# PSUM banks as single-bank tiles, constant rows behind the first layer norm, VectorE scores from three steps ahead

## Chip, cores, metric

The kernel runs on one core of a Trainium2 chip. The metric is the device time of one launch in microseconds (us). Each kernel is run several times. The median is quoted, and ratios are taken against runs of the kernel before, made in the same rounds on the same chip.

## The reference

A pre-norm transformer block: B = 1, S = 2048, D = 640, 32 heads of 20, gated width F = 1728, all in bf16.

```python
def _A_ref(x, wqkv, wo):                       # attention
    qkv = (x @ wqkv).reshape(B, S, 3, H, Dh).transpose(2, 0, 3, 1, 4)
    q, k, v = qkv[0], qkv[1], qkv[2]
    p = softmax(einsum("bhqd,bhkd->bhqk", q, k) * Dh ** -0.5)
    o = einsum("bhqk,bhkd->bhqd", p, v)
    return o.transpose(0, 2, 1, 3).reshape(B, S, D) @ wo

def _B_ref(x, w_gate, w_up, w_down):           # gated bilinear
    return ((x @ w_gate) * (x @ w_up)) @ w_down

h   = x + _A_ref(layernorm(x), A_wqkv, A_wo)
out = h + _B_ref(layernorm(h), B_w_gate, B_w_up, B_w_down)
```

## The kernel before

It has three stretches. The **start** normalises the first 512 rows, transposes them on TensorE and projects the first K and Q. **Attention** runs over five chunks of query rows. Scores go to PSUM three or two banks at a time, and ScalarE takes their exponential. One block in eleven (186 of 2048) goes instead to VectorE, which makes an exponential in four passes with one GpSimd pass beside them. Everything else (remaining projections, the output projection, second layer norm and gated stage of the chunk before) is filled in between by a planner in Python. The planner keeps modelled clocks `pe_t`, `dve_t`, `act_t` and decides the order of instructions. The **tail** is what is left of the last two chunks when the last exponential is done.

PSUM has eight banks. Outside attention the five score banks are lent to the other work as slices of two tiles:

```python
ring = deque([dict(t=0.0), dict(t=0.0)])           # the two ordinary banks, pool mp, tag "m"

def more_banks():                                  # before the first scores and after the last
    s3 = sA.tile([P, 3, BK], F32, name="sp", tag="s3")
    s2 = sA.tile([P, 2, BK], F32, name="sp", tag="s2")
    ap = [s3[:, i, :] for i in range(3)] + [s2[:, i, :] for i in range(2)]
    for i, a in enumerate(ap):
        ring.insert(i, dict(t=pe_t, ap=a))
# ... m_take() hands out the next ring entry: such a slice, or a new tile of mp
```

The start, in order of emission (cuts marked):

```python
for t_, r_, val in ((cstk, rowk, BIAS), (cstq, rowq, 1.0)):   # constant rows of K and Q
    nc.gpsimd.memset(t_[:], 0.0)
    nc.gpsimd.memset(t_[0:1, :], val)
    for ch in range(NCH):
        nc.gpsimd.dma_start(r_[:, ch, :], t_[:])
# ...
warm_up(28)                                   # 28 matmuls on zeros
# ...
for t in range(TPC):
    ln_stats(L, t, xt[0][:, t, :])            # VectorE
ln_finish(L)                                  # VectorE, then on GpSimd: den = (var + eps) ** 0.5
nc.vector.memset(Vx[...][:, :, :, DH], 1.0)   # three fills of V
nc.vector.memset(Vx[...], 0.0)
nc.vector.memset(Vx[...], 0.0)
# ... ScalarE copies the padded K and Q weights
ln_recip(L)                                   # VectorE waits for den
lns = [ln_apply(L, t, ...) for t in range(TPC)]
more_banks()
for t in range(TPC):
    run(transposed(lns[t], lnT_dst(t)))       # TensorE into a ring bank, copied out by ScalarE or VectorE
    warm_up(1)
warm_up(2)
run(proj_pad(0, 0, 1)); run(proj_pad(0, 0, 0))
less_banks()
```

The two settings of the order:

```python
LN_SLACK = 1.0    # us that a layer-norm transpose waits, in attention, after its planned input
D_STEPS = 2       # a VectorE score block is taken at least so many steps ahead of ScalarE's
```

In the tail the gate and up weights of the last chunk's tiles 0 to 7 are loaded early into memory that Q no longer needs. Tiles 8 to 13 go through a pool of three buffers, `wst`, so tile 11 needs the buffers of tile 8.

The softmax here doesn't subtract the row's maximum and nothing guards it: scores larger than these inputs give would overflow.

Of the kernel before, what the change touches and what calls it, by code (L numbers as in the profile page):

```python
# [10 lines left out]
F32 = mybir.dt.float32  # L11
# [4 lines left out]
PSUM = bass.MemoryType.PSUM  # L16

P = 128
# [8 lines left out]
BK = 512  # L27
NCH = S // BK
# [11 lines left out]
BIAS = 127.0 * UNIT  # L40
# [2 lines left out]
EXP_A = _P2 / _P3 * 65536.0  # L43
EXP_B = _P1 / _P3 * 65536.0 ** 2
EXP_C = UNIT * _P3 / 65536.0 ** 3
LN_SLACK = 1.0
D_V = 0.72
EPS_B = 1.0013580322265625e-05

# [3 lines left out]
BANK_ACT, FIX_ACT = 0.4267, 0.056  # L53
DVE_FIX = 0.12
D_AHEAD = 1.2
D_STEPS = 2
T_TICK = 3.41
HAM = 0.50
W0, W1 = 80.0, 58.0
# [13 lines left out]
def kernel(  # L73
# [11 lines left out]
    nc = tc.nc  # L85
# [14 lines left out]
    tiny = ctx.enter_context(tc.tile_pool(name="tiny", bufs=3))  # L100
    onp = ctx.enter_context(tc.tile_pool(name="onp", bufs=1))

    sA = ctx.enter_context(tc.tile_pool(name="sA", bufs=1, space=PSUM))
    accp = ctx.enter_context(tc.tile_pool(name="accp", bufs=1, space=PSUM))
    mp = ctx.enter_context(tc.tile_pool(name="mp", bufs=2, space=PSUM))


    pe_t = 0.0
# [30 lines left out]
    def dve(us, ready=0.0):  # L139
        nonlocal dve_t  # L140
        dve_t = max(dve_t, ready) + us + DVE_FIX
        return dve_t
# [67 lines left out]
    rowk = dram.tile([32 - DH, NCH, BK], BF16, name="rowk", tag="rowk")  # L210
    rowq = dram.tile([32 - DH, NCH, BK], BF16, name="rowq", tag="rowq")
    cstk = p1.tile([32 - DH, BK], BF16, name="cstk")
    cstq = p1.tile([32 - DH, BK], BF16, name="cstq")
    for t_, r_, val in ((cstk, rowk, BIAS), (cstq, rowq, 1.0)):
        nc.gpsimd.memset(t_[:], 0.0)
        nc.gpsimd.memset(t_[0:1, :], val)
        for ch in range(NCH):
            nc.gpsimd.dma_start(r_[:, ch, :], t_[:])

    def fill_kq():  # L220
        k_src = rowk[:].rearrange("r c q -> r (c q)")
# [26 lines left out]
    def ln_stats(L, i, s, ready=0.0):  # L248
        st = tiny.tile([P, 2, 6], F32, name="st", tag="st")
        for c in range(2):  # L250
            nc.vector.bn_stats(st[:, c, :], s[:, c * HD:(c + 1) * HD])
            dve(0.34, ready)
        nc.vector.bn_aggr(L["mv"][:, i, :], st[:])
        dve(0.15)

    def ln_finish(L):
        n = L["n"]
        vb = tiny.tile([P, TPC], BF16, name="vb", tag="vb")
        nc.vector.tensor_copy(vb[:, 0:n], L["mv"][:, 0:n, 1])
        ve = tiny.tile([P, TPC], BF16, name="ve", tag="ve")  # L260
        nc.vector.tensor_scalar_add(ve[:, 0:n], vb[:, 0:n], EPS_B)
        L["pow"] = dve(0.25)
        den = tiny.tile([P, TPC], BF16, name="den", tag="den")
        nc.gpsimd.tensor_tensor(den[:, 0:n], ve[:, 0:n], half[:, 0:n], ALU.pow)
        L["den"] = den
# [14 lines left out]

    ring = deque([dict(t=0.0), dict(t=0.0)])

    def more_banks():
        s3 = sA.tile([P, 3, BK], F32, name="sp", tag="s3")
        s2 = sA.tile([P, 2, BK], F32, name="sp", tag="s2")
        ap = [s3[:, i, :] for i in range(3)] + [s2[:, i, :] for i in range(2)]
        for i, a in enumerate(ap):
            ring.insert(i, dict(t=pe_t, ap=a))

    def less_banks():  # L290
        kept = [r for r in ring if "ap" not in r]
        ring.clear()
        ring.extend(kept)

    def m_wait():
        while ring[0]["t"] > pe_t + 0.05:
            yield ("until", ring[0]["t"])

    def m_take(dt=F32, shape=None):
        rec = ring.popleft()  # L300
        rec["t"] = NEVER
        ring.append(rec)
        if "ap" in rec:
            if shape is None:
                return rec["ap"], rec
            n = shape[1] * shape[2]
            return rec["ap"].bitcast(dt)[:, 0:n].rearrange("p (a b) -> p a b", b=shape[2]), rec
        t = mp.tile(shape or [P, BK], dt, name="mt", tag="m")
        return t[:], rec

    def m_done(rec, t):
# [27 lines left out]
    def transposed(ln_t, dst):  # L339
        ln, t = ln_t  # L340
        t += LN_SLACK if attn and left else 0.0
        while t + T_SEM > pe_t + 0.05:
# [97 lines left out]
    for t in range(TPC):  # L440
        ln_stats(L, t, xt[0][:, t, :])
    ln_finish(L)
    nc.vector.memset(Vx[:, :, 0:H * VS].rearrange("p t (h e) -> p t h e", e=VS)[:, :, :, DH], 1.0)
    nc.vector.memset(Vx[:, :, H * VS:VW], 0.0)
    nc.vector.memset(Vx[:, :, (H // 2) * VS:(H // 2) * VS + DH], 0.0)
# [12 lines left out]
    run(proj_pad(0, 0, 1))  # L458
    run(proj_pad(0, 0, 0))
    less_banks()  # L460

    def first_stage():
# [232 lines left out]
    for ci, qw in enumerate(CHUNKS):  # L695
# [3 lines left out]
        for g, k0 in order:  # L699
            k1 = k0 + TPC if ci == 0 and g < NG0 else NT  # L700
            n = (k1 - k0) * qw
# [80 lines left out]
    def start_D():  # L782
        used = {j for _, j in units[-1]}
        s0 = left[0][0] + D_STEPS
        for b in left:
# [42 lines left out]
    def pump(limit):  # L828

        while dq and dve_t < limit:  # L830
            ok = [d for d in dq if d["part"] < 3 or sum(b in E_of for b in eds) < 5]
            if not ok:
                return
            c = [d for d in ok if d["ready"] <= dve_t + 0.02]
            if not c:
                nxt = min(d["ready"] for d in ok)
                if nxt >= limit:
                    return
                c = [d for d in ok if d["ready"] == nxt]
            c.sort(key=lambda d: (d["part"] != 0, -d["part"]))  # L840
            pass_D(c[0])

    def emit_PV(s):
        nonlocal acc_t
        ci, q0, qw, g, pcs = steps[s]
        need(*[("V", z[0], g // (G // 2)) for z in pcs])
        k0, k1, first, last, full = ends[s]
        if first:
            acc_t = accp.tile([P, BK], F32, name="acc", tag="acc")
        for kt, qo, n, c in pcs:  # L850
            for j in range(HP):
                h = g * HP + j
                nc.tensor.matmul(acc_t[32 * j:32 * j + 32, qo:qo + n], lhsT=Vx[:, kt, h * VS:h * VS + 32],  # L853
                                 rhs=E_of[s, j][0][:, c:c + n], start=kt == k0, stop=kt == k1 - 1,
                                 skip_group_check=len(pcs) > 1)
        for j in range(HP):
            del E_of[s, j]
        pe(0.22, "C", 512)
        if last:
            before(pe_t + T_SEM)  # L860
            if (ci, g) not in sums:

                while sum(z[3] for z in later) > 1:
                    later.pop(0)[1]()
                sums[ci, g] = npool.tile([P, BK], F32, name="accS", tag="accS")
                nc.vector.tensor_copy(sums[ci, g][:, 0:qw], acc_t[:, 0:qw])  # L866
            else:
                nc.vector.tensor_tensor(sums[ci, g][:, 0:qw], sums[ci, g][:, 0:qw], acc_t[:, 0:qw], ALU.add)
            t = dve(qw / 960, pe_t + T_SEM)
            if full:  # L870
                normalise(ci, q0, qw, g, sums.pop((ci, g)), t)
            acc_t = None
# [64 lines left out]
    n = 0  # L937
# [5 lines left out]
    def v_time(s):  # L943
        return max(t_v.get((kt, steps[s][3] // (G // 2)), NEVER) for kt, *_ in steps[s][4])

    def values(force=None):

        nonlocal pv_next, bgw
        run = 0
        while pv_next < len(steps):  # L950
            s = pv_next
            if force is not None and s > force:
                break
            if not all((s, j) in E_of for j in range(HP)):
                if force is None:
                    break
                pump(dve_t + 0.5)
                continue
            if force is None and max([E_of[s, j][1] for j in range(HP)] + [v_time(s)]) > pe_t - MARG:
                break  # L960
            if force is None and run == 0 and not ends[s][3]:

                nxt = range(s, min(s + PVS, len(steps)))
                if not all((q, j) in E_of and max(E_of[q, j][1], v_time(q)) <= pe_t + 0.3 - MARG
                           for q in nxt for j in range(HP)):
                    break
            run += 1
            emit_PV(s)
            pv_next += 1
            ci, q0, qw, g, pcs = steps[s]  # L970
            if g == G - 1 and ends[s][4]:
                while len(bg) > (ci > 0):
                    forced()
                if ci == 0:
                    open_p2()
                    bgw = 0.0
                bg.append(second_stage(ci, q0, qw, xr_of(ci, q0, qw)))
                bgw += W1 * qw / BK
                if ci == len(CHUNKS) - 2:
                    load_last()  # L980

    while n < len(units):
# [6 lines left out]
        pe_t = max(pe_t, T0)  # L989
# [3 lines left out]
        if left:  # L993
            pe_t = max(pe_t, act_t + T_SEM)
# [21 lines left out]
        while True:  # L1016
            tick()
            if not blocked and bg and (pe_t < T1 + over and credit > 0 or debt >= BK):
                c0 = cols
                c = bg_step()  # L1020
                if isinstance(c, tuple):
                    blocked = c[1] > max(T1 + over, pe_t + 0.1)
                    pe_t = pe_t if blocked else max(pe_t, c[1])
# [12 lines left out]
        pump(act_t + 0.9)  # L1036
        n += 1
    values(len(steps))
    more_banks()
    while later:  # L1040
        later.pop(0)[1]()
    end = bg.pop()
    for c in end:
# [3 lines left out]
        elif isinstance(c, tuple):  # L1047
            while bg and pe_t < c[1]:
                forced()
            pe_t = max(pe_t, c[1])  # L1050
    wst.release()
    p2s.release()
    p2.release()


# [28 lines left out]
```

## Time and profile before

| | before |
|---|---|
| median (4 runs) | 1023.13 us (1021.88 to 1023.42) |
| first exponential starts | 21.64 us |
| last exponential ends | 960.0 us |
| tail to the end of the span | 64.0 us |
| ScalarE idle, 100 to 960 us | 68 us |
| gate/up loop of the last chunk | 23.4 us |

The busy lines of the page are busy us, share of the span and instructions. The slices cut the span in 40 and give tenths. PEclk is the clock granted to TensorE.

```profile
PE 869.5 (85%) x14138; PEld 369.7 (36%) x14138; DVE 748.1 (73%) x1294; ACT 862.3 (84%) x776; POOL 222.4 (22%) x264
...
PEclk9889898879989999989999899999989998999999
```

ScalarE and TensorE are both busy about 85% of the time, which says little. The stretches have different limits, so each is read by itself. Here is the start from the timeline: start, duration, engine, line, operation, out<-in, count, and in brackets how long the engine was idle before and what ended that.

```profile
2.02 9.05 PE L238 MATMUL acc<-zeros 128*128 128x512 bf16 x28
...
8.94 2.05 POOL L218 DMA_DIRECT2D rowq<-cstq  x4 [0.29 <-POOL cstq L216]
8.99 0.17 DVE L261 TENSOR_SCALAR ve<-vb 128x4 bf16<-128x4 bf16 x1
...
10.94 0.48 DVE L443 MEMSET Vx<- 128x512 bf16 x1 [1.79 <-issue]
11.00 1.06 POOL L264 TENSOR_TENSOR den<-ve,half 128x4 bf16<-128x4 bf16 x1
...
12.31 1.51 DVE L275 TENSOR_SCALAR xw<-xw,mv,rstd 128x640 bf16<-128x640 bf16 x4
...
12.81 0.45 PE L347 MATMUL sp<-ident,xw 128*128 128x128 bf16 x5 [1.73 <-DVE xw L275]
...
14.04 0.44 PE L347 MATMUL sp<-ident,xw 128*128 128x128 bf16 x5 [0.56 <-ACT lnT L322]
...
15.14 0.69 PE L347 MATMUL sp<-ident,xw 128*128 128x128 bf16 x5 [0.44 <-DVE lnT L326]
...
18.00 1.26 PE L148 MATMUL sp<-lnT,Wp 128*32 128x512 bf16 x20
...
21.64 4.62 ACT L776 ACTIVATE E<-sp 128x1536 bf16<-128x1536 f32 x4 [5.08 <-PE sp L757]
```

Two things stand out. The variance is ready at 9.16, but its power on GpSimd (`den`) starts at 11.00, behind the DMA issues for the constant rows. And the second and the third transpose begin just after the copy of the one before it has ended (at 13.99 and 15.08), although each writes another bank. The bracket names that copy as the releaser.

The same pattern fills the tail. The first fence is the list of waits of TensorE from 957 us on (total us, times, longest us): the first five of its eleven lines. The second is four lines of TensorE's timeline in the gate/up loop.

```profile
PE sp L148 <- ACT gs L322: 2.9, 6, 0.5
PE sp L148 <- DVE hh_4766 L671: 2.5, 2, 1.9
PE sp L148 <- DVE xr L685: 1.8, 3, 0.6
PE sp L148 <- DVE rb L885: 1.3, 1, 1.3
PE sp L148 <- DVE kT_155 L624: 1.2, 2, 0.6
```

```profile
992.61 0.73 PE L148 MATMUL sp<-kT_157,qT_164 128*32 128x256 bf16 x20 [0.59 <-DVE hh_4755 L671]
993.81 1.28 PE L148 MATMUL sp<-kT_157,qT_164 128*32 128x256 bf16 x40 [0.47 <-ACT gs L322]
995.61 0.73 PE L148 MATMUL sp<-kT_157,qT_164 128*32 128x256 bf16 x20 [0.52 <-ACT gs L322]
996.15 1.28 PE L148 MATMUL mt<-kT_157,qT_164 128*32 128x256 bf16 x40
```

`sp` is a slice of one of the two shared tiles, `mt` one of the two ordinary banks. In the second fence three groups into `sp` waited about half a microsecond each for the copy out of a neighbour slice; the group into `mt` follows at once. From start to start the group at 992.61 takes 1.20 us, and the one at 995.61 takes 0.54. The Trainium skill (PSUM - Partial Sum Buffer, "PSUM bank collisions raise a hardware error") asks for semaphores by bank and quadrant. So the order between different banks is asked for by nothing but the tile that holds them.

### The profile page before, as it was taken

Reading aid. Unit: us, or ns where it says so; the run is one execution under the profiler, and the core shown is the slowest. Engines: PE = TensorE matmul, PEld = TensorE weight load, DVE = VectorE, ACT = ScalarE, POOL = GpSimd, SP = SyncE. Lnnn points to the kernel's source line nnn. Section 1 sums busy time; section 2 is a strip of 40 time slices with the busy share of each in tenths; the row PEclk is TensorE's granted clock in tenths of the full one; section 3 lists DMA queues with packets and bytes.
Section 4 is the critical chain, followed back from the end, with each engine's and each line's share of the span. In section 5 each row is a group of like instructions: output and inputs, shape, how many; then the busy total and the mean of one; then the engine's idle time right before and its main releaser. Section 6 shows DMA issues by size and latency. Waiting matters only on the chain.

```text
span 1024.0 us, 32973 instructions
## 1 busy us (share of the span) xinstructions
PE 869.5 (85%) x14138; PEld 369.7 (36%) x14138; DVE 748.1 (73%) x1294; ACT 862.3 (84%) x776; POOL 222.4 (22%) x264
## 2 busy tenths in 40 slices
PE   7778887989788889888988889899789996888886
PEld 3233233222223222223333333344334443344565
DVE  4564586858798788877787788997778896788532
ACT  3578795879899999989999999999769997999511
POOL 4000220212232222222321222232222231122000
PEclk9889898879989999989999899999989998999999
DMA  6310110101110232210011122210213305123222
GB/s 228 81 41 3 45 34 17 39 22 34 30 49 10 54 80 72 66 49 26 26 39 41 45 55 55 45 37 24 42 35 84 68 17 145 38 65 73 57 60 47
DMA packets 121916, 53.26 MB, mean 52 GB/s; under 512 B 98026, under 2 KB 117066, under 8 KB 121770
## 3 DMA queue, kind: packets, MB, share of 16 engines
q1 hardware_dynamic: 120794, 49.75, 20.1%
q8 instruction: 110, 1.80, 0.7%
q10 hardware_dynamic: 720, 1.31, 0.3%
q14 instruction: 36, 0.29, 0.1%
q0 software_dynamic: 256, 0.10, 0.0%
HBM read 43.47 MB, written 2.98 MB: 45 GB/s over the span
## 4 chain that ended last, share of the span: by engine, by line
ACT 34%; PE 26%; issue 19%; DVE 8%; DMA 6%; SPq 4%; POOL 3%; DVEq 0%; POOLq 0%; ACTq 0%
ACT E L776 34%; PE mt L148 10%; PE sp L757 7%; PE acc L853 4%; PE sp L148 3%; SPq L404 3%; DMA rb<-rd 3%; SPq L898 1%; DMA rs<-accS 1%; DVE fx L803 1%; DVE v L811 1%; POOL uc L806 1%; DVE v L809 1%; DMA rd<-rr 1%; DMA kT_157<-tmp 1%
## 5 line engine op out<-in xcount | busy, mean ns | idle before, releaser
L776 ACT ACTIVATE E<-sp 128x1536 bf16<-128x1536 f32 (+1 forms) x745 | 850.0, 1330 | 93.4 <-PE sp L757 67.1
L806 POOL TENSOR_SCALAR uc<-fx 128x512 f32<-128x512 uint16 x186 | 158.4, 852 | 553.5 <-DVE fx L803 541.7
L853 PE MATMUL acc<-E,Vx 128*32 128x256 bf16 (+3 forms) x2787 | 166.7, 324 | 6.4 <-DVE accS L866 6.4
L809 DVE SCALAR_TENSOR_TENSOR v<-fx 128x512 f32<-128x512 uint16 x186 | 151.2, 815 | 1.6
L803 DVE TENSOR_SCALAR fx<-mt 128x512 int32<-128x512 f32 x186 | 126.9, 683 | 34.0 <-PE mt L757 33.1
L811 DVE SCALAR_TENSOR_TENSOR v<-v,uc 128x512 f32<-128x512 f32 x186 | 129.4, 697 | 25.8 <-POOL uc L806 22.4
L814 DVE SCALAR_TENSOR_TENSOR ed<-fx,v 128x512 uint16<-128x512 int32 x186 | 133.1, 716 | 1.6
L853 PEld LDWEIGHTS <-Vx 128*32 128x32 bf16 x3072 | 58.9, 97 | 77.3 <-issue 72.0
L148 PE MATMUL mt<-ln2T,wu 128*32 128x512 bf16 (+1 forms) x1070 | 77.7, 365 | 1.0 <-DVE fx L803 0.6
L148 PE MATMUL mt<-ln2T,wg 128*32 128x512 bf16 (+1 forms) x1080 | 77.4, 362 | 0.7 <-DVE hh_4759 L671 0.3
L853 PE MATMUL acc<-ed,Vx 128*32 128x256 bf16 (+3 forms) x285 | 70.5, 319 | 0.9 <-DVE accS L866 0.8
L148 PE MATMUL acc<-zeros 128*32 128x512 bf16 x680 | 58.4, 398 | 0.0
L326 DVE COPY gs<-mt 128x512 f32<-128x512 f32 (+3 forms) x54 | 33.6, 622 | 11.4 <-PE mt L148 11.0
L148 PEld LDWEIGHTS <-wg 128*32 128x32 bf16 x1190 | 28.0, 96 | 31.5 <-issue 23.3
L148 PEld LDWEIGHTS <-wu 128*32 128x32 bf16 x1190 | 28.0, 97 | 31.2 <-issue 22.5
L757 PE MATMUL sp<-qT_164,kT_155 32*128 32x256 bf16 (+3 forms) x285 | 28.9, 296 | 9.8 <-ACT E L776 9.3
L866 DVE COPY accS<-acc 128x512 f32<-128x512 f32 (+2 forms) x40 | 23.3, 582 | 17.4 <-PE acc L853 15.3
L757 PE MATMUL sp<-qT_164,kT_159 32*128 32x256 bf16 (+3 forms) x290 | 27.5, 292 | 9.4 <-ACT E L776 9.0
L757 PE MATMUL sp<-qT_164,kT_157 32*128 32x256 bf16 (+3 forms) x290 | 28.0, 297 | 8.7 <-ACT E L776 8.2
L757 PE MATMUL sp<-qT_164,kT_158 32*128 32x256 bf16 (+3 forms) x287 | 28.8, 309 | 7.5 <-ACT E L776 7.2
L757 PE MATMUL sp<-qT_164,kT_156 32*128 32x256 bf16 (+3 forms) x293 | 29.3, 299 | 6.7 <-ACT E L776 6.0
L757 PE MATMUL sp<-qT_164,kT_161 32*128 32x256 bf16 (+3 forms) x290 | 28.3, 292 | 7.6 <-ACT E L776 6.7
(254 smaller groups left out, 1193.9 us busy)
## 6 DMA issues: line engine op xcount, KB each, us to landing
wg<-in_B_w_gate_dram SPq DMA_DIRECT2D x57, 160.0 KB
wu<-in_B_w_up_dram SPq DMA_DIRECT2D x57, 160.0 KB
rb<-rd SPq DMA_DIRECT2D x16, 256.0 KB
rb<-rd SPq DMA_DIRECT2D x16, 192.0 KB
out_dram<-xr SPq DMA_DIRECT2D x14, 160.0 KB
Wd<-in_B_w_down_dram SPq DMA_DIRECT2D x13, 160.0 KB
xr<-in_A_x_dram SPq DMA_DIRECT2D x2, 640.0 KB
qT_164<-in_B_w_gate_dram SPq DMA_DIRECT2D x4, 320.0 KB
```

The lines of the kernel that those rows point to most:

```text
L148: nc.tensor.matmul(out[j:j + 32], lhsT=lhsT[:, j:j + 32], rhs=rhs, start=start, stop=stop, **kw)
L326: nc.vector.tensor_copy(dst, src)
L404: nc.sync.dma_start(dst, tmp[lo - ft * P:hi - ft * P, 0:n])
L757: nc.tensor.matmul(out[:, c:c + n], lhsT=kT[g][32 * j:32 * j + 32, kt * P:(kt + 1) * P], rhs=q_of(g, q0 + qo, n)[32 * j:32 * j + 32, :], s ...
L776: nc.scalar.activation(E[:, 0:len(u), :], sp[:, 0:len(u), :], ACT.Exp, scale=LN2_ / UNIT, bias=-BIAS * LN2_ / UNIT)
L803: nc.vector.tensor_scalar_mul(fx[:], d["sp"], 512.0)
L806: nc.gpsimd.tensor_scalar(d["uc"][:], u, EXP_C, 0.0, ALU.mult, ALU.add)
L809: nc.vector.scalar_tensor_tensor(d["v"][:], d["u"], EXP_A, d["u"], ALU.add, ALU.mult)
L811: nc.vector.scalar_tensor_tensor(d["v"][:], d["v"][:], EXP_B, d["uc"][:], ALU.add, ALU.mult)
L814: nc.vector.scalar_tensor_tensor(e[:], d["fx"][:], 1.0 / 512.0, d["v"][:], ALU.mult, ALU.add)
L853: nc.tensor.matmul(acc_t[32 * j:32 * j + 32, qo:qo + n], lhsT=Vx[:, kt, h * VS:h * VS + 32], rhs=E_of[s, j][0][:, c:c + n], start=kt == k0 ...
L866: nc.vector.tensor_copy(sums[ci, g][:, 0:qw], acc_t[:, 0:qw])
```

## The change

The intent is to lend the five banks as five tiles of their own pool, which is released before the score tiles are made and made anew after the last scores; to write the constant rows after the power of the first layer norm; and to retune the two settings of the order.

```diff
-LN_SLACK = 1.0
+LN_SLACK = 2.0
-D_STEPS = 2
+D_STEPS = 3
 ...
-    sA = ctx.enter_context(tc.tile_pool(name="sA", bufs=1, space=PSUM))
 ...
-    for t_, r_, val in ((cstk, rowk, BIAS), (cstq, rowq, 1.0)):
-        nc.gpsimd.memset(t_[:], 0.0)
-        ...
+    def const_rows():
+        for t_, r_, val in ((cstk, rowk, BIAS), (cstq, rowq, 1.0)):
+            nc.gpsimd.memset(t_[:], 0.0)
+            ...
 ...
+    sA = xp = None
     def more_banks():
-        s3 = sA.tile([P, 3, BK], F32, name="sp", tag="s3")
-        s2 = sA.tile([P, 2, BK], F32, name="sp", tag="s2")
-        ap = [s3[:, i, :] for i in range(3)] + [s2[:, i, :] for i in range(2)]
-        for i, a in enumerate(ap):
-            ring.insert(i, dict(t=pe_t, ap=a))
+        nonlocal xp
+        xp = tc.alloc_tile_pool(name="xp", bufs=1, space=PSUM)
+        for i in range(5):
+            ring.insert(i, dict(t=pe_t, tag=f"b{i}"))
     def less_banks():
 ...
+        xp.release()
+        sA = tc.alloc_tile_pool(name="sA", bufs=1, space=PSUM)
 ...  # in m_take()
-        if "ap" in rec:
-            ...
-        t = mp.tile(shape or [P, BK], dt, name="mt", tag="m")
+        pool, tag = (xp, rec["tag"]) if "tag" in rec else (mp, "m")
+        t = pool.tile(shape or [P, BK], dt, name="mt", tag=tag)
 ...
     ln_finish(L)
+    const_rows()
 ...
     values(len(steps))
+    sA.release()
     more_banks()
```

More of the change, by code (lines that the diff above doesn't have):

```diff
@@ L213 @@
     cstq = p1.tile([32 - DH, BK], BF16, name="cstq")
-    for t_, r_, val in ((cstk, rowk, BIAS), (cstq, rowq, 1.0)):
-        nc.gpsimd.memset(t_[:], 0.0)
-        nc.gpsimd.memset(t_[0:1, :], val)
-        for ch in range(NCH):
-            nc.gpsimd.dma_start(r_[:, ch, :], t_[:])
+    def const_rows():
+        for t_, r_, val in ((cstk, rowk, BIAS), (cstq, rowq, 1.0)):
+            nc.gpsimd.memset(t_[:], 0.0)
+            nc.gpsimd.memset(t_[0:1, :], val)
+            for ch in range(NCH):
+                nc.gpsimd.dma_start(r_[:, ch, :], t_[:])
     def fill_kq():
@@ L281 @@
     ring = deque([dict(t=0.0), dict(t=0.0)])
+    sA = xp = None
     def more_banks():
-        s3 = sA.tile([P, 3, BK], F32, name="sp", tag="s3")
-        s2 = sA.tile([P, 2, BK], F32, name="sp", tag="s2")
-        ap = [s3[:, i, :] for i in range(3)] + [s2[:, i, :] for i in range(2)]
-        for i, a in enumerate(ap):
-            ring.insert(i, dict(t=pe_t, ap=a))
+        nonlocal xp
+        xp = tc.alloc_tile_pool(name="xp", bufs=1, space=PSUM)
+        for i in range(5):
+            ring.insert(i, dict(t=pe_t, tag=f"b{i}"))
     def less_banks():
-        kept = [r for r in ring if "ap" not in r]
+        nonlocal sA
+        kept = [r for r in ring if "tag" not in r]
         ring.clear()
         ring.extend(kept)
+        xp.release()
+        sA = tc.alloc_tile_pool(name="sA", bufs=1, space=PSUM)
     def m_wait():
@@ L302, in m_take @@
         ring.append(rec)
-        if "ap" in rec:
-            if shape is None:
-                return rec["ap"], rec
-            n = shape[1] * shape[2]
-            return rec["ap"].bitcast(dt)[:, 0:n].rearrange("p (a b) -> p a b", b=shape[2]), rec
-        t = mp.tile(shape or [P, BK], dt, name="mt", tag="m")
+        pool, tag = (xp, rec["tag"]) if "tag" in rec else (mp, "m")
+        t = pool.tile(shape or [P, BK], dt, name="mt", tag=tag)
         return t[:], rec
@@ L1053 @@
     p2.release()
+    xp.release()
 _INS = ['A_x', 'A_wqkv', 'A_wo', 'B_x', 'B_w_gate', 'B_w_up', 'B_w_down']
```

## The prediction

> **What bounds the kernel now** (busy time by windows; timeline).
> - Start: the first exponential is at 21.64 us. Before it TensorE runs warm-up matmuls until 11.07, transposes four normalised tiles from 12.80, projects K and Q from 18.0.
> - Attention, about 100 to 960 us: ScalarE is 97 to 100% busy from 300 to 700; over the stretch it idles about 68 us, much of it in stalls of 5 to 7 us at chunk borders. 186 of 2048 score blocks go to VectorE.
> - Tail, 960 to 1024: ScalarE has almost nothing to do; TensorE, at full clock, is 74 to 82% busy and is the limit, with waits inside.
>
> **Single-bank tiles.** Banks 0-2 and 3-4 are slices of two tiles, and the trace shows waits that no data needs: a matmul group into one slice begins only when the copy out of the neighbour slice has ended.
> - Tail (waits of TensorE): twelve of 0.45 to 0.59 us in the gate/up loop and at its end, three of 0.59 before output groups, one of 1.95 behind a multiply which itself waits for the second layer norm, one of 0.50 at a transpose. With the matmul's drain each short one costs about 0.75. The gate/up loop takes 23.4 us (987.8 to 1011.15) for 28 groups of 0.545, that is 15.3: 8 us lost. The others are worth about 5. All 13 are on the critical path: TensorE alone carries the tail.
> - Given back: gate/up weights from tile 11 on wait for buffers that tile 8 frees; at 1.09 us a tile in place of 1.67 I estimate 2 us of waiting for them (issues are 1 us a tile apart). Net 11.
> - Start: transposes at 12.8, 14.0, 15.1, 16.05 each follow a copy. Without that they follow the four applies (1.51 us in all), and projection starts near 15: gain 2.5 to 3.
>
> The Trainium skill (PSUM - Partial Sum Buffer, PSUM bank collisions) asks for semaphores by bank, so separate banks need no order; these waits are wider.
>
> **Constant rows.** On GpSimd, four fills (0.51 us each) and eight DMA issues (4.35 us) stand before the power of the variance, which starts at 11.00 though its input is ready at 9.16: up to 1.8 us earlier. VectorE's fills of V, which also precede the reciprocal, start only at 10.94, a wait the profile calls issue; if that stays, the gain is hidden. I count 1. The moved issues now run beside applies and copies; the skill (SBUF - State Buffer, Who interferes with whom) says two-port VectorE modes and GpSimd descriptor writing block each other; no run here shows it yet; it may cost tenths. The rows are needed near 100 us: no effect there.
>
> **Three steps ahead; two us of slack for transposes.** Only order changes. A step takes about 2 us of ScalarE; a VectorE block takes four passes of 0.7 us plus a GpSimd pass, often two interleaved: two steps are tight, three comfortable. Matmuls wait directly for VectorE scores only 0.9 us, so the gain is smoother order: 0 to 6 us, with scatter from rearranged stalls. I count 2.
>
> **Sum.** 1023 - 11 - 4 - 2 = 1006 us; 8 in 10: 996 to 1016. Faster by over 2% (under 1002.6): 0.27; within 2%: 0.71; slower: 0.02.
>
> **Signs.** Last exponential to end 64 -> about 53 us; no TensorE wait for a copy of another bank, gate/up loop near 17 us, a new wait for weights. First exponential at 17.5 to 19. Power at 9.2 to 9.5. About 186 VectorE blocks; ScalarE idle of 100 to 960 within 10 us of 68.
>
> **What would make it wrong.** New stalls at chunk borders; weight arrival limiting the tail more; tracking that still joins the banks; a lower granted clock.

## The result

| | before | after |
|---|---|---|
| median (4 runs each) | 1023.13 us | 1010.29 us (1008.95 to 1014.04) |
| ratio | | 0.9883, 95% interval 0.9853 to 0.9912 |
| first exponential starts | 21.64 | 21.72 |
| first to last exponential | 938.4 | 935.3 |
| tail | 64.0 | 55.3 |
| gate/up loop | 23.4 | 17.8 |
| ScalarE idle, 100 us to the last exponential | 68 | 62 |
| VectorE blocks | 186 | 184 |

A ratio is the mean time of one kernel's runs over the mean of the other's of the same rounds, so not quite the ratio of the medians. The predicted 1006 us is 4 us low, and the measured time is inside the range. In the profiled run, which is the slowest of the four, the span falls by 11.7 us: 8.7 in the tail, 3.1 in attention, nothing in the start.

The page after:

```profile
PE 867.3 (86%) x14134; PEld 368.0 (36%) x14134; DVE 742.9 (73%) x1286; ACT 862.3 (85%) x777; POOL 219.8 (22%) x262
...
PEclk8779799899898989999999999999979999879999
```

The start after, from the timeline:

```profile
2.03 7.64 PE L239 MATMUL acc<-zeros 128*128 128x512 bf16 x28
...
9.16 0.17 DVE L262 TENSOR_SCALAR ve<-vb 128x4 bf16<-128x4 bf16 x1
...
9.41 1.03 POOL L265 TENSOR_TENSOR den<-ve,half 128x4 bf16<-128x4 bf16 x1 [5.48 <-DVE ve L262]
...
11.11 0.48 DVE L445 MEMSET Vx<- 128x512 bf16 x1 [1.79 <-issue]
...
12.18 1.54 DVE L276 TENSOR_SCALAR xw<-xw,mv,rstd 128x640 bf16<-128x640 bf16 x4
...
12.71 0.71 PE L348 MATMUL mt<-ident,xw 128*128 128x128 bf16 x5 [3.05 <-DVE xw L276]
...
13.65 0.74 PE L348 MATMUL mt<-ident,xw 128*128 128x128 bf16 x5
...
14.61 0.74 PE L348 MATMUL mt<-ident,xw 128*128 128x128 bf16 x5
...
17.52 2.85 PE L147 MATMUL mt<-lnT,Wp 128*32 128x512 bf16 x40
...
21.72 3.71 ACT L778 ACTIVATE E<-sp 128x1536 bf16<-128x1536 f32 x3 [5.64 <-PE sp L759]
```

The power now starts at 9.41, as intended, and the transposes no longer wait for copies: each follows the last warm-up matmul. Yet the first exponential has not moved. There are two reasons to test. The applies still start only at 12.18, because VectorE's fill of V starts at 11.11, after the same 1.79 us of "issue" as before. And the transposes and the matmuls between them are slow. The clock granted in this stretch shows it; the columns are length, busy time of PE, PEld, DVE, ACT, POOL, then the clock, DMA share and GB/s:

```profile
12.70:17.00 4.30, 3.19 (x24) 2.12 (x25) 1.79 (x6) 1.38 (x2) 0.00 (x0) 0.72 0.99 331
```

```profile
12.70:17.00 4.30, 4.29 (x26) 2.87 (x26) 2.00 (x5) 1.38 (x2) 3.95 (x8) 0.50 0.88 292
```

The grant fell from 0.72 (first line, before) to 0.50 (second line, after). In this execution the warm-up matmuls ended at 9.67, not 11.07, and TensorE then sat idle for 3.05 us. The warm-up is the same code in both kernels, so its earlier end is luck of this execution and no effect of the change. Windows of 0.5 us show where the clock of after falls and rises again:

```profile
11.50:12.00 0.50, 0.00 (x0) 0.00 (x0) 0.48 (x3) 0.00 (x0) 0.22 (x1) 0.77 1.07 364
...
18.50:19.00 0.50, 0.50 (x16) 0.20 (x10) 0.00 (x0) 0.00 (x0) 0.00 (x0) 0.90 0.29 98
```

It is 1.00 just before the first of these, 0.50 between them and 1.00 after the second. So TensorE had half the clock from about 11.8 to 18.5 us. In before the same windows give half the clock only from about 14.6 to 18.0. The skill (TensorE: Matmul & The Clock Gate, Part 1) describes a free-running window of about 3.4 us, half the clock after an idle window, and a phase that differs from run to run. The traces here agree on the half clock, on the phase that changes by chance, and on the length at the start (about 3.4 us in before, about twice that in after). They do not agree that a whole window must be idle: in after the clock fell about 2.1 us after the last warm-up matmul.

The waits of TensorE in the tail after:

```profile
PE mt L348 <- DVE xr L276: 3.0, 1, 3.0
PE mt L147 <- DMA wu<-in_B_w_up_dram: 1.4, 1, 1.4
PE mt L147 <- DVE on_346 L890: 1.1, 1, 1.1
```

No wait for the copy of another bank is left; the three that remain are for data. One is new: the transposes of the second layer norm, which TensorE used to reach late. Another is the predicted one, for gate/up weights. The third stands where before waited 1.3 us for the reciprocal `rb` to read a neighbour slice: TensorE now waits 1.1 us for the data that this reciprocal leads to, so little was gained at that place. The chain of waits from 982 us on (start, length, what) shows the same load:

```profile
981.88 9.14 PE mt L147 x324
...
991.05 3.48 PE mt L147 x120
...
994.55 4.59 DMA wu<-in_B_w_up_dram
...
999.18 9.46 PE mt L147 x258
```

The 4.59 us of the third line run from the issue of the load to its landing, not from when TensorE starts to wait. TensorE itself was idle 1.4 us before the matmuls of that tile, plus a few tenths before the groups ahead of it. The chain's length of a DMA is not the stall it causes.

### The profile page after: what moved, and what is told of

Read it like the earlier page. It is cut to its first block, busy times and chain, and to the rows that moved or that the text cites. A ratio compares the mean times of both kernels' runs of the same rounds, so it can differ in the third digit from the quotient of the medians.

```text
span 1012.3 us, 32948 instructions
## 1 busy us (share of the span) xinstructions
PE 867.3 (86%) x14134; PEld 368.0 (36%) x14134; DVE 742.9 (73%) x1286; ACT 862.3 (85%) x777; POOL 219.8 (22%) x262
## 4 chain that ended last, share of the span: by engine, by line
ACT 36%; PE 24%; issue 20%; DVE 9%; DMA 6%; SPq 4%; POOL 2%; DVEq 0%; POOLq 0%; ACTq 0%
ACT E L778 36%; PE mt L147 12%; PE sp L759 6%; PE acc L855 4%; SPq L405 3%; DVE fx L805 1%; DVE ed L816 1%; DMA rb<-rd 1%; DVE v L811 1%; DVE v L813 1%; DMA rd<-rr 1%; DMA rs<-accS 1%; POOL uc L808 1%; SPq L900 1%; PE acc L147 1%
## 5 line engine op out<-in xcount | busy, mean ns | idle before, releaser
L778 ACT ACTIVATE E<-sp 128x1536 bf16<-128x1536 f32 x746 | 850.0, 1343 | 90.9 <-PE sp L759 67.3
L808 POOL TENSOR_SCALAR uc<-fx 128x512 f32<-128x512 uint16 x184 | 155.4, 844 | 530.9 <-DVE fx L805 528.7
L855 PE MATMUL acc<-E,Vx 128*32 128x512 bf16 (+3 forms) x2791 | 167.5, 324 | 6.1 <-DVE Vx L327 3.4
L816 DVE SCALAR_TENSOR_TENSOR ed<-fx,v 128x512 uint16<-128x512 int32 x184 | 130.4, 710 | 1.3
L147 PE MATMUL mt<-ln2T,wu 128*32 128x512 bf16 (+1 forms) x1080 | 73.6, 356 | 1.8 <-DVE gs L327 1.6
L147 PE MATMUL acc<-zeros 128*32 128x512 bf16 x676 | 61.7, 424 | 0.0
L759 PE MATMUL sp<-qT_161,kT_152 32*128 32x256 bf16 (+3 forms) x281 | 28.6, 305 | 9.8 <-ACT E L778 9.5
L759 PE MATMUL sp<-qT_161,kT_154 32*128 32x256 bf16 (+3 forms) x290 | 28.6, 302 | 9.7 <-ACT E L778 9.0
L759 PE MATMUL sp<-qT_161,kT_155 32*128 32x256 bf16 (+3 forms) x287 | 30.0, 312 | 7.4 <-ACT E L778 7.2
L759 PEld LDWEIGHTS <-kT_154 32*128 32x128 bf16 x384 | 14.8, 93 | 59.1 <-issue 51.4
L759 PE MATMUL sp<-qT_161,kT_153 32*128 32x256 bf16 (+3 forms) x294 | 28.8, 297 | 7.4 <-ACT E L778 6.5
L759 PE MATMUL sp<-qT_161,kT_158 32*128 32x256 bf16 (+3 forms) x291 | 28.3, 293 | 7.0 <-ACT E L778 6.4
```

Of the source, the lines that this page charges most:

```text
L147: nc.tensor.matmul(out[j:j + 32], lhsT=lhsT[:, j:j + 32], rhs=rhs, start=start, stop=stop, **kw)
L759: nc.tensor.matmul(out[:, c:c + n], lhsT=kT[g][32 * j:32 * j + 32, kt * P:(kt + 1) * P], rhs=q_of(g, q0 + qo, n)[32 * j:32 * j + 32, :], s ...
L778: nc.scalar.activation(E[:, 0:len(u), :], sp[:, 0:len(u), :], ACT.Exp, scale=LN2_ / UNIT, bias=-BIAS * LN2_ / UNIT)
L808: nc.gpsimd.tensor_scalar(d["uc"][:], u, EXP_C, 0.0, ALU.mult, ALU.add)
L816: nc.vector.scalar_tensor_tensor(e[:], d["fx"][:], 1.0 / 512.0, d["v"][:], ALU.mult, ALU.add)
L855: nc.tensor.matmul(acc_t[32 * j:32 * j + 32, qo:qo + n], lhsT=Vx[:, kt, h * VS:h * VS + 32], rhs=E_of[s, j][0][:, c:c + n], start=kt == k0 ...
```

## The experiments

Twelve kernels ran, all correct, each with five rounds against the kernel before. Apart from names and line numbers, separate banks alone and moved rows alone leave TensorE's order exactly as before, and the two settings alone give TensorE's order of the changed kernel. So on TensorE banks and rows change waits only (the rows also move GpSimd's own work), and the settings change order only.

| run | what | median us | ratio to before, 95% | first exponential | first to last exponential | tail |
|---|---|---|---|---|---|---|
| banks_only | separate banks alone | 1012.98 | 0.9901 (0.9857 to 0.9945) | 20.70 | 937.3 | 55.1 |
| rows_only | moved rows alone | 1024.37 | 0.9985 (0.9953 to 1.0016) | 21.48 | 946.6 | 64.4 |
| steps_only | three steps alone | 1024.58 | 0.9994 (0.9959 to 1.0029) | 22.60 | 934.8 | 66.1 |
| slack_only | 2 us of slack alone | 1036.41 | 1.0128 (1.0083 to 1.0173) | 22.70 | 944.0 | 66.0 |
| steps_slack | both settings, no banks, no rows | 1023.02 | 0.9980 (0.9946 to 1.0014) | 21.54 | 934.1 | 65.1 |
| a_slack1 | after, slack back to 1 | 1010.90 | 0.9871 (0.9838 to 0.9905) | 20.55 | 930.5 | 55.2 |
| a_steps2 | after, steps back to 2 | 1022.25 | 0.9967 (0.9930 to 1.0004) | 21.55 | 940.8 | 53.8 |
| a_warm | after, longer warm-up | 1010.73 | 0.9860 (0.9835 to 0.9886) | 18.98 | 937.0 | 53.4 |
| a_vfill | after, V filled by GpSimd | 1007.91 | 0.9831 (0.9804 to 0.9859) | 19.58 | 934.1 | 55.7 |
| a_lastw | after, last weights wait for no buffer | 1010.47 | 0.9864 (0.9825 to 0.9903) | 20.63 | 936.0 | 51.8 |
| a_all | the three mends together | 1008.87 | 0.9837 (0.9801 to 0.9873) | 19.28 | 935.2 | 53.9 |
| after_again | the changed kernel again | 1008.72 | 0.9851 (0.9824 to 0.9878) | 20.11 | 932.3 | 53.6 |

The last three columns are from the one profiled execution of each. Four kernels shared a chip: banks_only to slack_only, then a_lastw, a_warm, a_vfill and a_slack1, then the other four.

A caution on these columns. The 33 timed runs of the kernel before spread from 1018.6 to 1030.2 us, and their time falls with the mean granted clock (correlation -0.82, about 5 us per 0.01 of clock). A single profile of the same program can thus be some us off in attention: rows_only has the order of before and shows 946.6 there, in a run of 1034.1 us that was the slowest of its seven. Parts of 1 or 2 us are settled here from the timeline, not from run times.

### Each part alone

**banks_only**, the diff of the change without its rows and settings.

> The kernel before with single-bank tiles alone; the order of instructions on every engine is that of before. Theory: the whole gain of the tail is here. Last exponential to the end of the span 64 -> 55.5 us, with one wait for late gate/up weights of up to 4.6 us in it; the start gains nothing in the first exponential (21.6 +- 0.5) because TensorE falls to half clock in the transposes after its idle gap; attention as before. Time 1014 to 1015. Rival (the gain in the tail came from the changed order): tail within 3 us of 64 and time 1020 or more. Second rival (the start was only unlucky in the one trace of after): first exponential at 18.5 to 19.5 and time 1011 to 1012.

Measured: tail 55.1, first exponential 20.70, ratio 0.9901, which is about 10 us. No wait for a neighbour's copy is left in the tail. The gain of the tail belongs to the banks, and the rival (order) falls: steps_slack has the order of the changed kernel and a tail of 65.1. The start gained about 1 us here, between the two theories.

**rows_only**

```diff
-    (constant rows before the warm-up)
     ln_finish(L)
+    const_rows()
```

> The kernel before with the constant rows moved alone; same order on all engines but GpSimd. Theory: nothing, because VectorE's fills of V start 1.8 us after the fill of the variance whatever GpSimd does, and stand before the reciprocal: the power starts at 9.2 to 9.5, the applies at 12.2 to 12.4, first exponential at 21.6 +- 0.4, time 1022 to 1024. Rival (the prediction's 1 us or more): applies near 10.6, first exponential at 19.5 to 20.6, time 1021 to 1022.

Measured: power at 9.44, but the fill of V at 11.14, applies at 12.21, first exponential at 21.48. The rows did what they were moved for, and nothing came of it in the start. The ratio's interval includes 1.

**steps_only** (`D_STEPS = 3`)

> The kernel before with VectorE scores three steps ahead alone. Tail and start as before (64 us after the last exponential). Theory: the gain of attention in the trace of after (938 -> 935 us from first to last exponential) is mostly this, so 1019 to 1021. Rival (the gain belongs to the slack of the transposes, or is scatter of rearranged stalls): 1022 to 1027.

**slack_only** (`LN_SLACK = 2.0`)

> The kernel before with two us of slack for the transposes alone. Tail and start as before. Theory: within 2 us of before, 1021 to 1025; its only purpose is at the chunk borders and first stage, where it exchanges waits of TensorE for later transposes. Rival (it carries the attention gain): 1018 to 1020.

Measured: steps alone gain nothing that can be told from 0, as the rival said (934.8 us in attention, but a tail 2 us longer in that trace), and slack alone loses 13 us by the ratio. The loss was expected by neither theory.

**steps_slack** and **a_steps2**

```diff
# steps_slack, against before
-LN_SLACK = 1.0
+LN_SLACK = 2.0
-D_STEPS = 2
+D_STEPS = 3
# a_steps2, against after
-D_STEPS = 3
+D_STEPS = 2
```

> The kernel before with both order settings (three steps, slack of 2 us), without banks and rows; TensorE's order is that of the changed kernel. Theory (the slack's loss of 1.3% is a property of one order, not of the slack, and is not there with three steps): ratio 0.996 to 1.002. Rival (costs add): 1.010 to 1.013.

> The changed kernel with the steps back at 2, so with the order of the slow slack-alone kernel, but separate banks and moved rows. Theory (three steps are what keeps the slack from costing, and banks are independent of it): ratio 0.999 to 1.005, 12 us or more over the changed kernel. Rival (separate banks or the moved start cure the slow order): ratio 0.987 to 0.992.

Measured: steps_slack 0.9980, as the theory said: with three steps the slack costs nothing. a_steps2, whose TensorE order is that of slack_only, came to 0.9967, below both of the theory's numbers by a little and above the rival's. Against after_again in the same rounds its mean is 1.17% longer (1020.5 against 1008.7 us, 11.8 us), near the expected 12. Where the slow order loses its time is the same in both: busy time from 500 to 700 us in slack_only, a_steps2, before and after, with the fourth number ACT's and the granted clock near the end:

```profile
500.00:700.00 200.00, 172.66 (x3014) 71.30 (x3006) 162.27 (x265) 187.59 (x165) 52.09 (x56) 0.95 0.18 42
```

```profile
500.00:700.00 200.00, 174.15 (x2991) 71.38 (x2987) 157.37 (x259) 183.32 (x161) 49.90 (x54) 0.91 0.18 41
```

```profile
500.00:700.00 200.00, 177.82 (x3215) 75.49 (x3217) 165.44 (x271) 196.59 (x174) 53.10 (x57) 0.97 0.18 42
```

```profile
500.00:700.00 200.00, 179.29 (x3296) 77.28 (x3294) 169.05 (x276) 199.23 (x177) 53.40 (x59) 0.99 0.19 45
```

ScalarE is busy 187.6 and 183.3 us there, against 196.6 and 199.2. The order with slack 2 and steps 2 leaves stalls of up to 3.6 us for ScalarE around one chunk border (526 to 564 us), and TensorE gets a lower clock around them. Why that combination and not the other three makes this border bad is not settled; it is a property of the planner's order, not of a cost of the slack.

**a_slack1** (`LN_SLACK = 1.0` in the changed kernel)

> The changed kernel with the slack of the layer-norm transposes back at 1 us. Alone the 2 us of slack cost 1.3% (ratio 1.0128). Theory (the two settings reshuffle stalls and do not add): ratio 0.986 to 0.991, like the changed kernel within 3 us. Rival (they add): 10 us or more under the changed kernel, ratio 0.978 or less.

Measured: 0.9871. With three steps the slack makes no difference that can be told. The settings do not add: 13 us for the slack at two steps, about 0 at three.

### Where the start's gain went

**a_warm**

```diff
     warm_up(28)
+    for _ in range(14):          # not counted by the planner, so its order stays
+        nc.tensor.matmul(pz[:], lhsT=zeros[:, 0:P], rhs=zeros[:], start=True, stop=True)
```

> The changed kernel with 14 more warm-up matmuls on zeros before the first transposes; nothing else moves. Theory (the start gained nothing because TensorE's idle gap of about 3 us before the first transpose is answered by half the clock, seen as 0.50 from 12.7 to 17): clock near 1.0 in 12.7 to 17, projection starts at 14.7 to 15.3, first exponential at 18.6 to 19.3, time 2 to 3 us under the changed kernel (ratio about 0.9855). Rival (the start is held by the copies and not by TensorE): projection at 17 or later whatever the clock.

```profile
12.70:17.00 4.30, 4.27 (x59) 2.59 (x61) 2.12 (x6) 1.39 (x2) 3.95 (x9) 1.00 0.89 293
```

Measured: clock 1.00, projection at 15.30 in place of 17.52, first exponential at 18.98 in place of 21.72. The theory holds: what held the start after the banks were separated was TensorE at half clock. After's own trace was an unlucky one, though: against the mean of five traces with its start, 20.9 (see below), the gain is 1.9 us. The time (0.9860) cannot be told from the changed kernel's.

**a_vfill**: the three `nc.vector.memset(Vx...)` become `nc.gpsimd.memset` behind the applies.

> The changed kernel with the three fills of V moved from VectorE, ahead of the reciprocal, to GpSimd behind the applies; TensorE's order is the same. Theory (the fills and the 1.79 us before them hid the earlier power): reciprocal at 10.5 in place of 12.0, applies from 10.7, first transpose at 11.2; first exponential 1.5 us earlier or more, 19.3 to 20.3. Rival (the wait belongs to whatever VectorE does next, or to descriptor writing on GpSimd): the reciprocal still starts near 12, first exponential at 21.7.

```profile
9.61 0.17 DVE L262 TENSOR_SCALAR ve<-vb 128x4 bf16<-128x4 bf16 x1
10.93 0.18 DVE L271 RECIPROCAL rstd<-den 128x4 f32<-128x4 bf16 x1 [1.16 <-POOL den L265]
11.15 1.79 DVE L276 TENSOR_SCALAR xw<-xw,mv,rstd 128x640 bf16<-128x640 bf16 x4
```

Measured: the reciprocal starts at 10.93 and now truly waits for the power; applies from 11.15, first exponential 19.58. The 1.79 us of "issue" belonged to the first fill of V and went with it. What it is, the traces don't say: it is 1.79 in every trace with that fill on VectorE.

**a_lastw**

```diff
-            wg = wst.tile([P, KC, P], BF16, name="wg", tag="wg")
+            own = end and f >= n_last + 3      # tiles 11 to 13 of the last chunk
+            if own:
+                kf = kT[f - n_last][:, 0:2 * KC * P].rearrange("p (w c f) -> p w c f", w=2, c=KC)
+            wg = kf[:, 0] if own else wst.tile([P, KC, P], BF16, name="wg", tag="wg")
 ...
-            wu = wst.tile([P, KC, P], BF16, name="wu", tag="wu")
+            wu = kf[:, 1] if own else wst.tile([P, KC, P], BF16, name="wu", tag="wu")
```

(A fourth buffer for `wst` did not fit the memory.)

> The changed kernel, with the gate/up weights of tiles 11 to 13 of the last chunk loaded into memory that the key tiles leave free after the last scores, so that they wait for no buffer; the order of instructions is otherwise that of the changed kernel. Theory (what the separate banks gained in the tail is partly given back to late weights): the 4.6 us from the issue of a weight load to its landing leave the chain of work that ended last, TensorE waits for no weight, tail 55.3 -> 50.5 to 52 us, time 4 us under the changed kernel (ratio to before about 0.984). Rival (the weights wait was slack, or the loads come late for another reason such as the queue): tail 54 to 55.5 and ratio 0.988.

```profile
PE mt L348 <- DVE xr L276: 3.0, 1, 3.0
PE mt L147 <- DVE on L893: 1.1, 1, 1.1
```

Measured: no wait for weights, tail 51.8. But the tail of the changed kernel is 55.3 in one trace and 53.6 in another (after_again), so only 1.8 of the difference is the weights. The other 1.7 is the clock after TensorE's 3.0 us wait for the second layer norm. The same stretch after that wait in after and in a_lastw, 14 us each:

```profile
971.00:985.00 14.00, 14.00 (x384) 10.84 (x380) 3.75 (x8) 0.49 (x2) 0.00 (x0) 0.88 0.09 32
```

```profile
970.60:984.60 14.00, 14.00 (x444) 11.59 (x440) 4.21 (x9) 1.25 (x4) 0.00 (x0) 1.00 0.15 48
```

The grant is 0.88 in the first and 1.00 in the second and in after_again: the same idle gap is or is not answered by half clock for a while. Three more traces with the same order and the same 3.0 us gap fit. With the weights wait the tail is 53.6 and 53.4 at full clock after the gap (after_again, a_warm) and 55.3 and 55.7 with the low clock (after, a_vfill); without the weights wait it is 51.8 and 53.9 (a_lastw, a_all). Times again don't separate a_lastw (0.9864) from the changed kernel.

**a_all**, the three together, and **after_again** in the same rounds:

> The changed kernel with all three mends together: 14 more warm-up matmuls, fills of V on GpSimd, last weights in free memory. Theory (the start and the tail are the places where the change's gain was held back, and the three add): first exponential at 17.5 to 18.5, tail 50.5 to 52.5, attention as in the changed kernel; time 6 to 8 us under the changed kernel in the same rounds, ratio to before 0.979 to 0.983. Rival (the start does not propagate through the first stage, or the tail waits for something else): within 4 us of the changed kernel.

> The changed kernel itself once more, on the chip of the others: ratio 0.986 to 0.991.

Measured: means 1007.2 against 1008.7 us, so 1.5 us, not 6 to 8; the rival was right. The mends do not add. The 14 more warm-up matmuls end at about 13, so the first transpose starts at 12.99 although its input is ready near 11: the longer warm-up ate what the earlier power had won, and the first exponential is at 19.28. In the tail there is no wait for weights, but this trace drew the 0.88 clock after the layer norm's gap. No version beats the changed kernel by an amount that can be told; a_vfill has the lowest ratio (0.9831), on another chip than after_again (0.9851), with overlapping intervals.

## Why the prediction was right or wrong

- **Tail, gross 13 us: right.** At full clock and without the weights wait it went from 64.0 to 51.8 us, 12.2. The gate/up loop was predicted near 17 us and took 17.8. The waits were for tile neighbours, as banks_only shows.
- **2 us given back to late weights: right.** 1.8 us between after_again and a_lastw.
- **Net tail 11 us: 10.4 (after_again) or 8.7 (after).** The missing part of the second is a half-clock patch after a wait of TensorE for the second layer norm, which the prediction did not have.
- **Start from banks, "gain 2.5 to 3": wrong.** This is the step that failed. The waits did go, but the prediction let the transposes keep pace with the four applies and left out TensorE's clock, which is halved around the gap before them. (It also read the fourth transpose as held by a copy, which it was not.) In five traces with the start of the changed kernel (after, after_again, a_lastw, a_slack1, a_steps2) the first exponential is at 20.1 to 21.7 us, against 21.5 to 22.7 in before, steps_only, slack_only and steps_slack: 20.9 against 22.1 in the mean, about 1.2 for banks and rows together where 4 were counted. That the pair shows no gain at all is luck: before drew a half clock of about 3.4 us and after one of about 6.8. Where it lasted about 3.4 us the first exponential is at 20.1 to 20.6 (after_again, a_slack1, a_lastw) against 21.5 to 21.6 (before, steps_slack); where it lasted about 6.8 us, at 21.6 to 21.7 (after, a_steps2) against 22.6 to 22.7 (steps_only, slack_only). The gain is 1.0 to 1.2 us either way. a_warm, at full clock, shows the lost part.
- **Rows, "I count 1": 0 in the start.** The named doubt held: the fills of V hid it (rows_only, a_vfill). The feared cost of tenths to the applies did not come: the four took 1.54 us against 1.51. The first group of issues took 2.55 us against 2.30.
- **Settings, "I count 2": the size held, at 0.9980 with an interval that includes 0.** The reason given, smoother order, is not shown. That order can cost 12 us either way (slack_only, a_steps2) was only covered by the word scatter.
- **Sum.** By runs: banks 10 us, both settings 2, rows 1.5, each from its ratio and each with an interval of 3 us or more to either side. 17 predicted, 12 to 15 measured (0.9883 and 0.9851); the miss is mostly the start.
- **Signs.** Power at 9.41: right. First exponential 17.5 to 19: wrong. VectorE blocks 184 and ScalarE idle 62 us: right.

## What to carry to other kernels

Where independent buffers are slices of one tile, look in the waits for a writer of one slice released by a reader of another: on the critical engine each cost about 0.7 us here (1.20 us from start to start in place of 0.54), and separate tiles removed them without touching the order. Before counting a gain in a stretch that starts behind an idle TensorE, read the granted clock there; a shorter wait elsewhere can leave the gap, and the half clock, in place. Settings of a planner that only change order must be tried together, since one that loses 1.3% alone can cost nothing beside another.

## What the Trainium skill lacked or had wrong

- TensorE: Matmul & The Clock Gate, Part 1 puts the loss of clock at an idle window of about 3.4 us. At the start of after the clock fell about 2.1 us after the last warm-up matmul had ended at 9.67. In before it fell at about 14.6, after a gap of 1.73 us and then two transposes with a gap of 0.56 between them. A reader needs the warning that TensorE can lose the clock without a whole idle window.
- SBUF - State Buffer, "Who interferes with whom" says that the second to issue blocks fully. It gives no size for a fill beside a normalising pass. Where a fill on GpSimd overlapped the four applies (a_vfill), one of them took 0.72 us and the other three about 0.44; a one-row fill took 0.63 us against 0.51. That is one instruction held for about 0.3 us, which does not contradict the page; no run shows the mode that VectorE was in.
- No page explains the 1.79 us before the strided fill of V (128 x 512 elements, bf16) on VectorE, which the profile calls issue and which is the same in every trace that has it.
